# Fused attention and expert layer: the experts' products in a fixed order, the last batch's end and the first expert's entry in smaller pieces

## The chip, the core and the metric

The kernel runs on one core of one Trainium2 chip. Times are device microseconds of one execution; the metric is the median over several executions. The core's engines run side by side and wait for each other through semaphores: PE (TensorE, the matrix products; its weight loads are shown apart as PEld), DVE (VectorE), ACT (ScalarE), POOL (GpSimd) and SP (SyncE, which here only issues transfers). Transfers run on 16 DMA engines.

## What is computed

Attention over 8 batches with 8 heads, 576 positions and 64 numbers per head, masked by blocks of 64, and behind it a layer of 8 experts. Each of the 4608 tokens goes to the expert with the largest logit; of an expert's tokens only the 80 with the largest gate are kept, and all other output rows are zero.

```python
scores = 1.0 / np.sqrt(D) * np.matmul(q, k.transpose(0, 1, 3, 2))
scores = np.where(block_i >= block_j, scores, -1e9)
attn = np.exp(scores - scores.max(-1, keepdims=True))
attn = attn / (attn.sum(-1, keepdims=True) + 1e-09)
x = np.matmul(attn, v).transpose(0, 2, 1, 3).reshape(B * S, H * D)
...
logits = x @ w_gate
expert_idx = np.argmax(logits, axis=1)
gate_w = softmax(logits)[np.arange(N), expert_idx]
for e in range(E):
    tok_idx = np.where(expert_idx == e)[0]
    if len(tok_idx) > capacity:
        keep = np.argpartition(-gate_w[tok_idx], capacity)[:capacity]
        tok_idx = tok_idx[keep]
    h = np.maximum(x[tok_idx] @ w1[e], 0.0)
    out[tok_idx] = gate_w[tok_idx, None] * (h @ w2[e])
```

## The kernel before

The attention takes two heads (a pair) at a time, 32 turns in all. Four pairs make a batch. What each turn issues on each engine is written out by hand in the lists `TURN`, and for the last turn `LAST` (lines 40 and 139): scores on PE, row maxima on DVE, exponentials on ACT, transposes of the probabilities on PE (`back`, in the groups A, B and C), copies out of the PSUM banks (`take`), and the products with v (`values`, lines 683 to 707), which go to the tiles `V0` (eight of nine blocks) and `V1`. The results of four pairs lie transposed in `xT`. `flip` turns them into `Y`, which SP stores to DRAM, and `logits_of` (line 399) multiplies them with the gate's weights, on four column groups of PE at once. `logits_out` copies the logits with ACT, `logits2` transposes them, `products` multiplies them with the reciprocal softmax sums and adds over the heads, `shift`, `expo`, `first_of` and `weight` find each token's expert and gate, and `turn`, `turn2` and `placed` write the gates by expert into `Wt`. For earlier batches this runs beside the next turns. For the last one it stands by itself (lines 829 to 863).

Then DVE takes the largest gates of each partition and half (`MAX8`, line 889). PE spreads them within an expert (line 913), DVE counts for one half how many are larger (line 958), ACT for the other (line 961), which gives each candidate its slot. One-hot tiles `OH` (line 966) and products with the row numbers (line 979) give a table `gi`, by which POOL gathers the rows of each expert (`xg`, line 993).

Per expert, `prepare` divides the rows by their sums (line 1091, four pieces on DVE), transposes them on PE (line 1111) and copies them with ACT (line 1112). `first` makes the first layer (line 1102, two halves of 32 products, two records each), `second` the second (line 1155), and POOL scatters the rows to the output (line 1164). The order in which PE gets this part is not written out: the program's scheduler sets it, apart from a chain within each `second`. `finish` computes the gates' table and a check sum that must hold before the first scatter.

`warm` (line 724) issues products that nothing reads, so that PE is not idle: the numbers in `WARM`, 12, 6, 9 and 24 of them, stand behind `turn2` of batches 6 and 7, behind the ranking, and behind the products with the row numbers. SP clears the output with 18 transfers of 512 KB (`clear`): four in each of the last turns, 16 in all, and two more among the weights. Weights come as 16 transfers of 2 MB into nine buffers; three are loaded during the attention, the fourth when the last batch is stored, the fifth to ninth behind the second gather (`fetches[HOLD]`), the rest as buffers come free.

Of the kernel before, what the change touches and what calls it, by code (L numbers as in the profile page):

```python
# [18 lines left out]
P = 128  # L19
BLK = 64  # L20
NT = 5
FW0, FWA, FWC, FWB = 3, 3, 1, 2
WARM = [8, 12, 6, 9, 24]
# [114 lines left out]
LAST_BANKS = {"B": (4, 5), "A": (0, 1), "C": (6, 7), "L": (2,), "av": (3,)}  # L138
# [17 lines left out]
    (0, "take", "C1", "v"),  # L156
    (0, "values"),
# [12 lines left out]
def tile_attn_moe(ctx, tc, q, k, v, w_gate, w1, w2, capacity, out, xs=None, dbg=None):  # L170
# [77 lines left out]
    prod = sm1.tile([P, NT, H, E], F32, name="prod")  # L248
    lgT = sm1.tile([P, NT * P], F32, name="lgT")
# [108 lines left out]
    class Batch:  # L358
# [18 lines left out]
        def flip(self, pr):  # L377

            nc.vector.transpose(self.Y[:, :, pr], self.xT[:, pr])
# [16 lines left out]
        def logits(self):  # L396
            self.logits_out(self.logits_of())

        def logits_of(self):
            lt = banks("g")  # L400
# [7 lines left out]
        def logits_out(self, lt):  # L408
            for c in range(2):
                nc.scalar.copy(lgT[:, BLK + 288 * c:BLK + 288 * (c + 1)], lt[c][:, 0:288])  # L410
# [9 lines left out]
        def products(self):  # L420
            for pr in range(NP):
                iv = self.la[pr // 2][:, 0:BLK * NT].rearrange("p (t r c) -> p t r c", t=NT, r=2)[:, :, pr % 2, 0:2 * E]
                yield nc.vector.tensor_tensor(
                    prod[:, :, 2 * pr:2 * pr + 2], iv.rearrange("p t (s e) -> p t s e", s=2),
# [4 lines left out]
            yield nc.vector.tensor_reduce(self.lg, prod.rearrange("p t h e -> p t e h"), axis=AX.X, op=ALU.add)  # L429
# [21 lines left out]
        def weight(self):  # L451
            vec = nc.vector
            N = NT
            g = sm.tile([P, N], F32, name="g", bufs=2)
# [54 lines left out]

        def turn2(self, tp):  # L510
# [24 lines left out]
    class Pair:  # L535
# [147 lines left out]
        def values(self):  # L683

            (av,), (self.last,) = banks("av", self.where), banks("L", self.where)
            a4 = self.last[:, 4 * BLK:5 * BLK]
            if turns:
# [4 lines left out]
                     (1, 1, 0, 1, None), (1, 2, 1, 2, 2), (2, 2, 2, 6, 4), (3, 3, 3, 6, 5)]  # L692
            for n_, (j, row, b0, b1, c0) in enumerate(steps):
                for h in range(2):
                    r = slice(h * D, (h + 1) * D)
                    nc.tensor.matmul(a4[r] if c0 is None else av[r, BLK * c0:BLK * (c0 + b1 - b0)], lhsT=self.vn[:, h, j, :],  # L696
                                     rhs=self.PT[:, h, row, b0:b1].rearrange("p b r -> p (b r)"),
                                     start=(n_ < 2), stop=False)
            for h in range(2):
                r = slice(h * D, (h + 1) * D)  # L700
                nc.tensor.matmul(a4[r], lhsT=self.vn[0:BLK, h, 2, :], rhs=self.PT[0:BLK, h, 2, 0], start=False, stop=True)  # L701
                nc.tensor.matmul(av[r, 7 * BLK:8 * BLK], lhsT=self.vt[BLK:P, h, :], rhs=self.PT[BLK:P, h, 2, 0],
                                 start=False, stop=True)
            xT = self.bt.xT[:, self.pr].rearrange("p (b r) -> p b r", r=BLK)
            self.out["V0"] = (bass.AP(xT.tensor, xT.offset, [xT.ap[0], [5 * BLK, 2], [1, 4 * BLK]]),
                              av.rearrange("p (i c) -> p i c", i=2))
# [29 lines left out]
    cleared, kept = 0, 2  # L736
# [55 lines left out]
    slots_ = dict(pe=pe, t=t, ta=ta, warm=lambda: warm(START_WARM, banks("L")[0]))  # L792
# [3 lines left out]
    with tc.manual_schedule():  # L796
        warm(WARM[0], banks("g")[0])
        early = loads(FW0)
        for i in range(-LEAD, n):
# [6 lines left out]
            for _ in range(min(4, nz - kept - cleared) if i >= n - 5 else 0):  # L806
# [51 lines left out]
        for g_ in (found, found, found, weighed, found, weighed, weighed):  # L858
            next(g_)
        bt.turn(nc.vector, 2)  # L860
# [45 lines left out]
    for h in (1, 0):  # L906
# [478 lines left out]
```

## Time and profile before

| | before |
|---|---|
| median of 3 runs | 395.24 us (393.61 to 395.93) |
| the profiled execution | 398.6 us |
| span of the profiled execution | 396.9 us |
| PE busy | 374.6 us (94%) |
| DVE, ACT, POOL busy | 279.5, 289.9, 185.0 us |
| moved by DMA | 84.42 MB |

The span runs from the first to the last instruction of the program; the execution's own time is 1.7 us longer. Times within the profile count from the span's start. [...]

### The profile page before, as it was taken

What the parts mean: (1) busy time and instruction counts of PE and PEld (TensorE: products, weight loads), DVE (VectorE), ACT (ScalarE), POOL (GpSimd) and SP (SyncE); (2) the same over time, 40 slices, a digit from 0 to 9 for tenths busy, and PEclk for the clock granted to TensorE, in tenths of its full rate; (3) what the DMA queues carried; (4) which work ended last, traced back from release to release, by engine and by line L of the source; (5) the groups of instructions that cost most, each with busy time, mean ns of one, the idle gap of its engine ahead of it and who ended that gap; (6) DMA issues with size and microseconds to landing.
All of it is one profiled execution on the core that took longest, in us unless ns stands there. A gap on an engine that the chain in (4) does not pass through costs nothing.

```text
span 396.9 us, 15142 instructions
## 1 busy us (share of the span) xinstructions
PE 374.6 (94%) x5963; PEld 254.3 (64%) x5963; DVE 279.5 (70%) x787; ACT 289.9 (73%) x886; POOL 185.0 (47%) x383
## 2 busy tenths in 40 slices
PE   5899999998999999999999999998996999999991
PEld 3666666665766766766676667666675955655541
DVE  5879899997999999999999999999743230100010
ACT  1799999998999999999999999996121223333231
POOL 6246665674965877667695556301146001000010
PEclk9999999999999999999999999999997899999997
DMA  9969999898999999999999998997669999999401
GB/s 124 153 120 191 145 182 176 160 216 106 190 244 174 155 179 195 161 172 197 128 166 220 154 144 192 385 405 223 144 224 274 391 400 397 393 397 390 182 18 40
DMA packets 169919, 84.42 MB, mean 213 GB/s; under 512 B 132573, under 2 KB 151869, under 8 KB 169840
## 3 DMA queue, kind: packets, MB, share of 16 engines
q1 hardware_dynamic: 158352, 61.80, 71.8%
q0 software_dynamic: 9120, 21.27, 23.2%
q8 instruction: 49, 0.80, 1.0%
q10 hardware_dynamic: 2368, 0.30, 0.6%
q14 instruction: 30, 0.25, 0.3%
HBM read 63.21 MB, written 20.33 MB: 211 GB/s over the span
## 4 chain that ended last, share of the span: by engine, by line
PE 81%; DVE 7%; DMA 4%; issue 3%; SPq 1%; ACT 1%; ACTq 0%; POOL 0%; POOLq 0%; DVEq 0%
PE bank L597 20%; PE bank L696 18%; PE bank L678 13%; PE ps L1102 10%; PE av L1155 9%; DMA ld<-in_q_dram 2%; PE bank L403 2%; PE bank L701 2%; SPq L558 1%; PE bank L614 1%; DMA ld<-in_k_dram 1%; DVE raw L633 1%; DVE negm L633 1%; PE bank L417 1%; PE pm L1155 1%
## 5 line engine op out<-in xcount | busy, mean ns | idle before, releaser
L644 ACT ACTIVATE P<-bank,negm 128x512 f32<-128x512 f32 (+3 forms) x320 | 158.4, 584 | 10.4 <-DVE negm L633 8.0
L597 PE MATMUL bank<-T,qt 64*128 64x320 f32 (+3 forms) x512 | 99.4, 496 | 0.6 <-DVE PT L714 0.6
L633 DVE TENSOR_REDUCE negm<-bank 128x1 f32<-128x320 f32 (+2 forms) x192 | 83.5, 473 | 11.1 <-PE bank L623 11.1
L696 PE MATMUL bank<-PT,vn 128*64 128x64 f32 (+3 forms) x1280 | 88.1, 293 | 0.6 <-ACT PT L714 0.6
L714 ACT COPY PT<-bank 128x512 f32<-128x512 f32 x158 | 81.9, 652 | 3.1 <-PE bank L678 2.6
L696 PEld LDWEIGHTS bank<-PT,vn 128*64 128x64 f32 x1280 | 56.3, 137 | 27.1 <-ACT PT L714 5.2
L580 POOL TENSOR_SCALAR qt<-T 128x128 f32<-128x128 f32 (+2 forms) x96 | 31.1, 342 | 88.5 <-DVE T L573 88.5
L644 ACT ACTIVATION_READ_ACCUMULATOR P<-bank,negm 128x1 f32 x256 | 70.6, 277 | 0.0
L678 PEld LDWEIGHTS bank<-ident,P 64*128 64x128 f32 (+1 forms) x1600 | 58.5, 137 | 11.7 <-issue 6.4
L678 PE MATMUL bank<-ident,P 64*128 64x64 f32 (+1 forms) x1600 | 64.1, 225 | 1.1 <-ACT P L644 0.6
L597 PEld LDWEIGHTS bank<-T,qt 64*128 64x128 f32 x512 | 47.9, 187 | 26.5 <-ACT PT L714 15.6
L633 DVE TENSOR_REDUCE raw<-bank 128x1 f32<-128x64 f32 (+1 forms) x128 | 51.6, 441 | 2.5 <-PE bank L597 1.6
L573 DVE STREAM_TRANSPOSE T<-ld 128x576 f32<-128x576 f32 x64 | 49.3, 770 | 5.0 <-DMA ld<-in_q_dram 3.7
L566 POOL DMA_DIRECT2D vn<-in_v_dram x58 | 46.0, 796 | 1.2 <-issue 1.1
L1102 PE MATMUL ps<-xsT,w 128*64 128x80 f32 x1024 | 41.7, 241 | 3.7 <-issue 3.1
L1102 PEld LDWEIGHTS ps<-xsT,w 128*64 128x64 f32 x1024 | 39.2, 143 | 7.7 <-issue 6.3
L1164 POOL DMA_INDIRECT out_dram<-y,si x8 | 7.4, 924 | 77.9 <-DVE y L1159 77.9
L1159 DVE SCALAR_TENSOR_TENSOR y<-av,comb,yt 80x512 f32<-80x512 f32 (+1 forms) x8 | 5.6, 696 | 50.5 <-ACT yt L1158 50.5
L558 POOL DMA_DIRECT2D ld<-in_k_dram x54 | 37.4, 702 | 4.5 <-DMA ld<-in_q_dram 3.1
L1155 PE MATMUL av<-w,hT 128*32 128x512 f32 (+2 forms) x320 | 39.0, 553 | 0.0
L1125 ACT ACTIVATE hT<-ps 128x320 f32<-128x320 f32 x16 | 7.0, 438 | 35.4 <-PE ps L1102 35.4
L1158 ACT ACTIVATE yt<-ps,gfar 32x512 f32<-32x512 f32 (+2 forms) x18 | 11.4, 636 | 24.5 <-PE ps L1155 24.3
(190 smaller groups left out, 437.7 us busy)
## 6 DMA issues: line engine op xcount, KB each, us to landing
w<-in_moe_w_dram SPq DMA_DIRECT2D x13, 2048.0 KB, 20.6
xs<-Y SPq DMA_DIRECT2D x32, 288.0 KB, 6.4
out_dram<-zero SPq DMA_DIRECT2D x18, 512.0 KB, 7.3
ld<-in_q_dram SPq DMA_DIRECT2D x126, 72.0 KB, 5.3
vn<-in_v_dram POOLq DMA_DIRECT2D x58, 128.0 KB, 5.5
ld<-in_k_dram SPq DMA_DIRECT2D x72, 72.0 KB, 5.4
w<-in_moe_w_dram POOLq DMA_DIRECT2D x8, 512.0 KB, 7.4
ld<-in_k_dram POOLq DMA_DIRECT2D x54, 72.0 KB, 6.4
```

The source lines that it names most:

```text
L558: eng.dma_start(self.nat[x][r], (q, k)[x][b, h0 + h, :, 32 * i:32 * i + 32] .rearrange("(g r) d -> r g d", r=32))
L566: eng.dma_start(self.vn[:, h], v[b, h0 + h, 0:512].rearrange("(j p) d -> p j d", p=P))
L573: nc.vector.transpose(t, self.nat[x].rearrange("p g d -> p (g d)"))
L580: nc.gpsimd.tensor_scalar(qb[:, to], tb[:, of], scalar1=SCALE, scalar2=1.0, op0=ALU.mult, op1=ALU.mult)
L597: nc.tensor.matmul(s[h][:, c:c + n], lhsT=q_[:, P * t - BLK:P * t + BLK], rhs=k_[:, 0:n], start=(c == 0 and g != "2"), stop=(g == "1"))
L633: nc.vector.tensor_reduce(to[:, b, h:h + 1], self.s[g][h][:, c:c + n], axis=AX.X, op=ALU.max, negate=True)
L644: nc.scalar.activation(Pt[self.i % 2][u][:, h, c1:c1 + n], self.s[g][h][:, c:c + n], AF.Exp, bias=self.negm[:, t, h:h + 1], scale=1.0, acc ...
L678: nc.tensor.transpose(pt[c][0:cols.stop - cols.start, n_ * BLK:(n_ + 1) * BLK], row[u][r, h, cols], ident[r, r])
L696: nc.tensor.matmul(a4[r] if c0 is None else av[r, BLK * c0:BLK * (c0 + b1 - b0)], lhsT=self.vn[:, h, j, :], rhs=self.PT[:, h, row, b0:b1]. ...
L714: (nc.scalar.copy if (eng or TAKE[x]) == "a" else nc.vector.tensor_copy)(*self.out.pop(x))
L1102: yield nc.tensor.matmul(dst(b)[64 * c:64 * (c + 1)], lhsT=w_[:, a, col:col + 64], rhs=x_[:, a], start=(a == 0), stop=(a == n - 1))
L1155: last = nc.tensor.matmul(to[col:col + s1 - s0, c0:c1], lhsT=hT[:, a, s0:s1], rhs=w_[:, a, c0:c1], start=(a == ends[0]), stop=(a == ends[1 ...
```

## The change

It does these things:

- PE's order in the expert part is fixed: each `first` follows the `second` of two experts before, each `second` follows the `first` of the next expert. The check sum's second product stands behind the first `second`.
- The first expert enters in four pieces: each is divided, transposed and copied into a tile of its own, and the first half of its products goes piece by piece.
- In the last batch the logits of three of four pairs are made before the values; `V0` lies in two banks, copied by ACT and DVE at once; the logits' second half is copied by DVE; `flip` is cut in two. The products are written with the head innermost (`prod_`). Batch 6's `placed` goes to ACT. `turn_gated` multiplies gate and one-hot in another order, and the tile `Gm` of the last batch is written by POOL.
- The ranking begins with the half that DVE counts.
- All 18 clears go into the last turns, up to five each. Of the five weight loads behind the second gather, the third to fifth each wait for the load two before.
- `WARM` is 9, 6, 9 and 21 in place of 12, 6, 9 and 24. A loop that only runs when the check sum fails gets 30 passes in place of 28.

PE at the first expert's entry; `xn` are the divided rows, `xsT` and `x_0` to `x_3` the transposed ones, `ident` marks a transpose. Before:

```order
L724 MATMUL ps_6160<-identr 128x512 x24
L1111 MATMUL pm<-ident,xn 128x80 x4
L1102 MATMUL ps<-xsT,w 64x80 x32
L1111 MATMUL pm<-ident,xn 128x80 x4
L1102 MATMUL ps<-xsT,w 64x80 x32
```

With the change:

```order
L753 MATMUL ps_6171<-identr 128x512 x21
L1181 MATMUL pm<-ident,xn_0_6241 128x80
L1181 MATMUL pm<-ident,xn_1_6242 128x80
L1181 MATMUL pm<-ident,xn_2_6243 128x80
L1144 MATMUL ps<-x_0_6237,w 64x80 x8
L1181 MATMUL pm<-ident,xn_3_6244 128x80
L1157 MATMUL ps<-x_0_6237,w 64x80 x2
L1144 MATMUL ps<-x_1_6238,w 64x80 x8
L1144 MATMUL ps<-x_2_6239,w 64x80 x8
L1144 MATMUL ps<-x_3_6240,w 64x80 x8
L1167 MATMUL pm<-ident,xn 128x80 x4
```

The first eight products need only the first piece, and two products of the second half have moved between them.

PE at the last batch's values (`PT` and `vn`), logits (`wgd`) and their transposes (`lgT`). Before:

```order
L696 MATMUL bank_5875<-PT,vn 64x256 x2
L696 MATMUL bank_5875<-PT,vn 64x192 x2
L701 MATMUL bank_5876<-PT,vn 64x64
L702 MATMUL bank_5875<-PT,vt_147 64x64
L701 MATMUL bank_5876<-PT,vn 64x64
L702 MATMUL bank_5875<-PT,vt_147 64x64
L403 MATMUL bank_5927<-xT,wgd 32x288 x4
L403 MATMUL bank_5928<-xT,wgd 32x288 x4
L417 MATMUL bank_5946<-ident,lgT 128x64
```

With the change:

```order
L404 MATMUL bank_5878<-xT,wgd 32x288 x3
L404 MATMUL bank_5879<-xT,wgd 32x288 x3
L721 MATMUL bank_5886<-PT,vn 64x64 x2
L721 MATMUL bank_5887<-PT,vn 64x256 x2
...
L726 MATMUL bank_5888<-PT,vn 64x64
L727 MATMUL bank_5887<-PT,vt_148 64x64
L404 MATMUL bank_5878<-xT,wgd 32x288
L404 MATMUL bank_5879<-xT,wgd 32x288
L418 MATMUL bank_5955<-ident,lgT 128x64
```

Six of the eight logits products stand ahead of the values now, and two behind.

The diff, cut to its core:

```diff
-WARM = [8, 12, 6, 9, 24]
+WARM = [8, 9, 6, 9, 21]
...
-LAST_BANKS = {"B": (4, 5), "A": (0, 1), "C": (6, 7), "L": (2,), "av": (3,)}
+LAST_BANKS = {"B": (4, 5), "A": (0, 1), "C": (6, 7), "L": (2,), "av": (3, 4), "g": (5, 0)}
...
+    (0, "logits"),
     (0, "values"),
...
-        def flip(self, pr):
-
+        def flip(self, pr, g0=0, g1=S // 32):
+            nc.vector.transpose(self.Y[:, g0:g1, pr], self.xT[:, pr, 32 * g0:32 * g1])
...
+        def logits_of(self, lt, prs=range(NP)):
             for c in range(2):
-                for pr in range(NP):
+                for pr in prs:
...
+        def logits_out(self, lt, cs=range(2), copy=None):
+            for c in cs:
+                (copy or nc.scalar.copy)(lgT[:, BLK + 288 * c:BLK + 288 * (c + 1)], lt[c][:, 0:288])
...
+            by_head = prod if self.b < B - 1 else prod_.rearrange("p t e h -> p t h e")
...
-                    prod[:, :, 2 * pr:2 * pr + 2], iv.rearrange("p t (s e) -> p t s e", s=2),
+                    by_head[:, :, 2 * pr:2 * pr + 2], iv.rearrange("p t (s e) -> p t s e", s=2),
...
-            yield nc.vector.tensor_reduce(self.lg, prod.rearrange("p t h e -> p t e h"), axis=AX.X, op=ALU.add)
+            yield nc.vector.tensor_reduce(self.lg, by_head.rearrange("p t h e -> p t e h"), axis=AX.X, op=ALU.add)
...
+        def turn_gated(self):
+            self.sp = sp = sm.tile([P, E, NT, 8], F32, name="sp", bufs=1)
+            gs = sm.tile([P, NT, 8], F32, name="gs", bufs=1)
+            nc.vector.tensor_tensor(gs, self.g.unsqueeze(2).broadcast_to([P, NT, 8]),
+                                    sameE.unsqueeze(1).broadcast_to([P, NT, 8]), op=ALU.mult)
+            eq = self.eq.rearrange("p t e -> p e t")
+            for s_ in range(2):
+                nc.vector.tensor_tensor(
+                    sp[:, s_:E:2], eq[:, s_:E:2].unsqueeze(3).broadcast_to([P, E // 2, NT, 8]),
+                    gs.unsqueeze(1).broadcast_to([P, E // 2, NT, 8]), op=ALU.mult)
+            nc.gpsimd.tensor_tensor(Gm[:, NT * self.b:NT * (self.b + 1)], self.eq,
+                                    self.g.unsqueeze(2).broadcast_to([P, NT, E]), op=ALU.mult)
...
-            yield nc.vector.tensor_copy(Wt[:, :, :, self.b, :].rearrange("p h t a -> p t a h"),
-                                        self.tp[:, 0:8 * NT].rearrange("p (t a h) -> p t a h", t=NT, h=2))
+            yield (nc.scalar.copy if self.b == B - 2 else nc.vector.tensor_copy)(
+                Wt[:, :, :, self.b, :].rearrange("p h t a -> p t a h"),
+                self.tp[:, 0:8 * NT].rearrange("p (t a h) -> p t a h", t=NT, h=2))
...
+            two = len(avs) > 1
...
+            if two:
+                steps = [y for j, row, b0, b1, c0 in steps for y in (
+                    [(j, row, b0, b0 + 4 - c0, c0), (j, row, b0 + 4 - c0, b1, 4)]
+                    if c0 is not None and c0 < 4 < c0 + b1 - b0 else [(j, row, b0, b1, c0)])]
...
+            if two:
+                self.out.update((f"V0{i}", (self.bt.xT[:, self.pr, 5 * BLK * i:5 * BLK * i + 4 * BLK],
+                                            avs[i][:, 4 * BLK * i:4 * BLK * (i + 1)])) for i in range(2))
...
-    cleared, kept = 0, 2
+    cleared, kept = 0, 0
...
+    def logits():
+        early_logits.extend(banks("g", LAST_BANKS))
+        batches[B - 1].logits_of(early_logits, range(NP - 1))
...
-            for _ in range(min(4, nz - kept - cleared) if i >= n - 5 else 0):
+            for _ in range(min(5, nz - kept - cleared) if i >= n - 5 else 0):
...
-        to, from_ = pairs[n - 1].out.pop("V0")
         pairs[n - 1].take("V1", "v")
-        nc.scalar.copy(to[:, 0], from_[:, 0])
-        nc.vector.tensor_copy(to[:, 1], from_[:, 1])
+        pairs[n - 1].take("V00", "a")
+        pairs[n - 1].take("V01", "v")
...
-        lt = bt.logits_of()
-        pairs[n - 1].flip()
+        bt.logits_of(early_logits, (NP - 1,))
+        bt.flip(NP - 1, 0, S // 64)
+        bt.logits_out(early_logits, (0,))
+        bt.logits_out(early_logits, (1,), nc.vector.tensor_copy)
+        bt.flip(NP - 1, S // 64, S // 32)
-        bt.logits_out(lt)
...
-        bt.turn(nc.vector, 2)
+        bt.turn_gated()
...
-    for h in (1, 0):
+    for h in range(2):
...
+    hot = vec.tensor_tensor(slot[:, 0:NH], cnt_v, pen[:, 0], op=ALU.add)
+    for c0 in range(0, NCAND, 3):
+        if c0 == NH:
+            with tc.issue_after(hot.ins):
+                hot = vec.scalar_tensor_tensor(slot[:, NH:], cnt_a, 0.5, pen[:, 1], op0=ALU.mult, op1=ALU.add)
+        with tc.issue_after(hot.ins):
...
+        parts = finish_()
...
+        yield
+        pc2 = ps_m.tile([P, 512], F32, name="pm")
+        with tc.issue_after(added_[0].ins):
+            nc.tensor.matmul(pc2[:, 0:1], lhsT=ones, rhs=dsb, start=True, stop=True)
         vec.tensor_tensor(nb, nb, pc2[:, 0:1], op=ALU.add)
...
-    weights(1, fetches[HOLD])
-    with tc.issue_after(loaded.ins):
-        while cleared < nz:
-            loaded = clear(cleared, nc.sync)
-            cleared += 1
-    weights(FWA - 2 + FWC + FWB, fetches[HOLD])
+    assert cleared == nz or ov is None
+    behind = [fetches[HOLD], fetches[HOLD]]
+    for _ in range(FWA - 1 + FWC + FWB):
+        weights(1, behind.pop(0))
+        behind.append(loaded.ins)
...
+        if pieces is not None:
+            for a in range(n):
+                pieces(a, after)
+                for b in range(nb):
+                    for c in range(2):
+                        col = (2 * b + c) * 64
+                        with ExitStack() as order:
+                            if after is not None:
+                                order.enter_context(tc.issue_after(after.ins))
+                            after = nc.tensor.matmul(dst(b)[64 * c:64 * (c + 1)], lhsT=w_[:, a, col:col + 64],
+                                                     rhs=x_[a], start=(a == 0 and b == 0),
+                                                     stop=(a == n - 1 and b == nb - 1))
+                yield after
+            return
...
+    def prepare_pieces():
+        x_ = [fx.tile([P, CHUNK], F32, name=f"x0_{a}") for a in range(KP)]
+        xn = [fx.tile([CHUNK, P], F32, name=f"xn0_{a}") for a in range(KP)]
+        divide(xn, xg[0])
+        def turn_(a, after):
+            tp = ps_m.tile([P, 512], F32, name="pm")
+            with ExitStack() as order:
+                if after is not None:
+                    order.enter_context(tc.issue_after(after.ins))
+                nc.tensor.transpose(tp[:, 0:CHUNK], xn[a], ident[0:CHUNK, 0:CHUNK])
+            nc.scalar.copy(x_[a], tp[:, 0:CHUNK])
+        def pieces(a, after):
+            for a_ in range(3) if a == 0 else range(a + 2, min(a + 3, KP)):
+                turn_(a_, after)
...
+        turned_[e] = last
...
-        last = None
+        last = turned_[min(e + 1, E - 1)]
...
+        added_[e] = last
...
+        pieces = None
+        if e == 0:
+            xs_[0], pieces = prepare_pieces()
+        elif e + 1 < E:
+            ready(e + 1)
...
-            hT_[e] = first(e, xs_[e], (lambda: ready(1)) if e == 0 else None)
+            hT_[e] = first(e, xs_[e], (lambda: ready(1)) if e == 0 else None, added_.get(e - 2), pieces)
...
-            finish(divided_[2])
+            rest = finish(divided_[2])
...
-            scatter(e - 1, second(e - 1, hT_[e - 1]))
+            y = second(e - 1, hT_[e - 1])
+            for _ in rest if e == 1 else ():
+                pass
+            scatter(e - 1, y)
```

## Rows read from the trace of the kernel before

**Rows 1.** The page, busy time of each engine

```profile
PE 374.6 (94%) x5963; PEld 254.3 (64%) x5963; DVE 279.5 (70%) x787; ACT 289.9 (73%) x886; POOL 185.0 (47%) x383
```

**Rows 2.** Timeline of PE, last batch: start us, us, engine, line, op, out<-in, xcount [idle before]

```profile
274.59 2.75 PE L696 MATMUL bank<-PT,vn 128*64 128x320 f32 x40 [0.63 <-ACT PT L714]
...
277.95 1.34 PE L403 MATMUL bank<-xT,wgd 128*32 128x288 f32 x16 [0.33 <-DVE xT L714]
```

**Rows 3.** Timeline of PE, first experts

```profile
292.03 5.73 PE L724 MATMUL ps<-identr 128*128 128x512 f32 x24
...
298.56 2.06 PE L1102 MATMUL ps<-xsT,w 128*64 128x80 f32 x43 [0.52 <-ACT xsT L1112]
301.77 0.29 PE L1102 MATMUL ps<-xsT,w 128*64 128x80 f32 x2 [1.16 <-issue]
...
304.63 1.35 PE L1102 MATMUL ps<-xsT,w 128*64 128x80 f32 x16 [0.41 <-issue]
...
306.63 4.09 PE L1102 MATMUL ps<-xsT,w 128*64 128x80 f32 x64
...
311.08 4.65 PE L1102 MATMUL ps<-xsT,w 128*64 128x80 f32 x128
```

**Rows 4.** Waits of PE, 296 to 320: line, releaser, us in total, times, longest

```profile
PE ps L1102 <- issue: 3.1, 4, 1.2
```

**Rows 5.** Stretches: us, busy PE, PEld, DVE, ACT, POOL (records), granted clock, DMA share, GB/s

```profile
302.00:304.00 2.00, 0.49 (x4) 0.38 (x3) 0.00 (x0) 0.00 (x0) 1.60 (x5) 0.82 1.05 408
...
306.00:310.00 4.00, 4.00 (x54) 3.83 (x56) 0.89 (x4) 0.86 (x2) 0.00 (x0) 0.50 1.04 334
...
360.00:370.00 10.00, 10.00 (x223) 7.53 (x217) 0.74 (x1) 3.35 (x6) 0.91 (x1) 1.00 1.04 388
370.00:380.00 10.00, 10.00 (x145) 4.88 (x143) 0.75 (x1) 2.92 (x5) 0.91 (x1) 1.00 0.22 76
```

**Rows 6.** DMA queues (transfers, MB, share): the page, then 303 to 305

```profile
q8 instruction: 49, 0.80, 1.0%
...
q8 instruction: 1, 0.02, 3.0%
```

**Rows 7.** Timeline of DVE, last batch to first expert

```profile
269.23 1.40 DVE L633 TENSOR_REDUCE negm<-bank 128x1 f32<-128x320 f32 x4
...
280.31 0.68 DVE L423 TENSOR_TENSOR prod<-bank,rs 128x80 f32<-128x80 f32 x4 [0.96 <-PE bank L417]
281.03 0.82 DVE L429 TENSOR_REDUCE lg<-prod 128x40 f32<-128x320 f32 x1
...
282.24 0.22 DVE L521 COPY Wt<-bank 128x40 f32<-128x40 f32 x1
...
288.25 0.42 DVE L958 TENSOR_SCALAR_CACHE_REDUCE junk<-av,key 128x192 bf16<-128x192 f32 x1 [0.95 <-PE av L913]
...
290.48 1.36 DVE L966 TENSOR_TENSOR OH<-slot,iota_s 128x240 bf16<-128x240 f32 x4
...
296.52 0.89 DVE L1091 TENSOR_TENSOR xn<-xg 80x128 f32<-80x128 f32 x4 [4.13 <-DMA xg<-xs,gi]
```

**Rows 8.** Timeline of ACT, ranking and first expert

```profile
287.41 0.42 ACT L961 ACTIVATE junk<-ps,keyn 128x192 bf16<-128x192 f32 x1 [4.82 <-DMA xs<-Y]
...
289.71 0.23 ACT L961 ACTIVATION_READ_ACCUMULATOR junk<-ps,keyn 128x1 f32 x1
...
298.08 0.43 ACT L1112 COPY xsT<-pm 128x320 f32<-128x320 f32 x1 [5.50 <-issue]
```

**Rows 9.** Timeline of SP's transfers

```profile
246.53 20.11 SPq L239 DMA_DIRECT2D out_dram<-zero  x16
...
277.72 0.38 SPq L387 DMA_DIRECT2D xs<-rs  x1
...
283.56 15.19 SPq L337 DMA_DIRECT2D w<-in_moe_w_dram  x2
```

**Rows 10.** Chain that ended last: start us, us, what

```profile
378.15 0.44 PE pm L1155 x2
```

More of the change, by code (lines that the diff above doesn't have):

```diff
@@ L683, in values @@
         def values(self):
-            (av,), (self.last,) = banks("av", self.where), banks("L", self.where)
+            avs, (self.last,) = banks("av", self.where), banks("L", self.where)
+            two = len(avs) > 1
             a4 = self.last[:, 4 * BLK:5 * BLK]
@@ L692, in values @@
                      (1, 1, 0, 1, None), (1, 2, 1, 2, 2), (2, 2, 2, 6, 4), (3, 3, 3, 6, 5)]
+            first = {2: two}
+            if two:
+                steps = [y for j, row, b0, b1, c0 in steps for y in (
+                    [(j, row, b0, b0 + 4 - c0, c0), (j, row, b0 + 4 - c0, b1, 4)]
+                    if c0 is not None and c0 < 4 < c0 + b1 - b0 else [(j, row, b0, b1, c0)])]
+            low = [n_ for n_, x in enumerate(steps) if x[4] is not None and x[4] < 4][-1] if two else None
             for n_, (j, row, b0, b1, c0) in enumerate(steps):
@@ L1060, in finish_ @@
         vec.tensor_reduce(nb, pc[:, E:E + 2], axis=AX.X, op=ALU.add)
-        pc2 = ps_a.tile([P, 512], F32, name="av")
-        nc.tensor.matmul(pc2[:, 0:1], lhsT=ones, rhs=dsb, start=True, stop=True)
+        yield
+        pc2 = ps_m.tile([P, 512], F32, name="pm")
+        with tc.issue_after(added_[0].ins):
+            nc.tensor.matmul(pc2[:, 0:1], lhsT=ones, rhs=dsb, start=True, stop=True)
         vec.tensor_tensor(nb, nb, pc2[:, 0:1], op=ALU.add)
@@ L1112, in prepare, with first @@
         nc.scalar.copy(x_.rearrange("p a s -> p (a s)"), tp[:, 0:KP * CHUNK])
-        return x_, last
-    def first(e, x_, then=None):
+        return [x_[:, a] for a in range(KP)], last
+    def prepare_pieces():
[4 more added lines that the diff above has]
+            tp = ps_m.tile([P, 512], F32, name="pm")
+            with ExitStack() as order:
+                if after is not None:
+                    order.enter_context(tc.issue_after(after.ins))
+                nc.tensor.transpose(tp[:, 0:CHUNK], xn[a], ident[0:CHUNK, 0:CHUNK])
[3 more added lines that the diff above has]
+                turn_(a_, after)
+        return x_, pieces
+    def first(e, x_, then=None, after=None, pieces=None):
         hT = fx.tile([P, FP, CHUNK], F32, name="hT", bufs=3)
@@ L1119, in first @@
             ph = ps_s.tile([P, 512], F32, name="ps")
-            for last in blocks(lambda b: ph[:, b * CHUNK:(b + 1) * CHUNK], w_[:, :, 512 * f:512 * (f + 1)], x_, KP, 4):
+            for last in blocks(lambda b: ph[:, b * CHUNK:(b + 1) * CHUNK], w_[:, :, 512 * f:512 * (f + 1)], x_, KP, 4,
+                               None if f else after, None if f else pieces):
                 pass
@@ L1151, in second @@
                                         (far[i][1], rest[far[i][0]], FAR, (NEAR, FP - 1)))
-                    with ExitStack() as order:
-                        if last is not None:
-                            order.enter_context(tc.issue_after(last.ins))
+                    with tc.issue_after(last.ins):
                         last = nc.tensor.matmul(to[col:col + s1 - s0, c0:c1], lhsT=hT[:, a, s0:s1], rhs=w_[:, a, c0:c1],
@@ L1210, in tile_attn_moe @@
         step = 1.0
-        for it in range(28):
+        for it in range(30):
             vec.tensor_scalar(mid, lo, scalar1=step, scalar2=None, op0=ALU.add)
```

59 lines of the change are left out of this document (25 added, 34 removed).

## The prediction

> **What bounds the kernel now.** I read the page first: PE is busy for 374.6 of 396.9 us [rows 1], so only time in which PE does nothing useful, or works slowly, can be won. Up to 274 us the change leaves PE's order alone, so I went on to the timeline of PE from the last batch to the first experts. There the reader should see two things. First, a chain without overlap: the last values products (from 274.59), the logits (277.95), their transposes, DVE's choice of an expert, the ranking, the gather, and the 24 filling products that only keep PE working (292.03 to 297.76) [rows 2, 3]. The first product of an expert starts at 298.56. Second, that this expert runs badly. Its 128 matmul records should take what the next expert's 128 take, 4.65 us. They take 7.42 (298.56 to 305.98) and 4.09 for the two halves of 64 [rows 3]. Against 2.32 for each half that is 5.10 + 1.77 = 6.9 us lost.
>
> The waits of PE say that 3.1 us of it are four gaps with no releaser that the profile shows ("issue") [rows 4]. [...] The DMA engines, meanwhile, are full (share 1.05) from 302. The queue view offers a suspect: the queue of kind "instruction" moved 49 transfers, 0.80 MB, so 16 KB each, and one of them falls into 303 to 305, where the gaps end; the same view of 283 to 303 lists none [rows 6]. From 311 PE is dense to the end (10.00 of 10 us at 360 to 370). The weights are not what it waits for: the DMA share falls to 0.22 at 370 to 380 [rows 5], so the last weights land near 372, and the last expert's products on them begin at 378.15 [rows 10], some 6 us later.
>
> **The change part by part.** Shifts are us earlier (+) or later (-) for the first expert.
>
> Early logits. Three of four head pairs' logits, 12 of 16 records, move ahead of the values. The 16 took 1.34 us, so 12 cost about 1.0. PE stands idle 0.63 us there, waiting for ACT's copy of PT; about 0.4 sticks out and moves the values [rows 2]. Behind the values only two logits products remain, but both write the same 32 rows of their banks, and I count them one after the other, so the second half is no earlier relative to the values. The transposes go into banks of their own now: four of ten no longer wait for the second copy, 0.15 to 0.2 gained. DVE's copy of the second half stands between two halves of the flip, and the second flip ends before the transposes do. Net -0.2 (bounds -0.5 and +0.2).
>
> The products of the last batch are written with the head innermost. The sum over heads read every eighth number and took 0.82 us for 320 numbers; a reduction of 320 neighbours took 0.35 (1.40 for four) [rows 7]. That is +0.45 if writing costs nothing, and 0 if the four products (0.68 together) pay what the sum saves; I take +0.25. [...]
>
> The copy of batch 6's places goes from DVE to ACT: its row has 0.22 us there, half of it beside the next one [rows 7], +0.1. ACT is idle there. The product with the gate is not removed from DVE: gs takes the place of Gm, so 0; Gm itself goes to POOL, where nothing waits for it.
>
> Ranking: the half that DVE counts goes first. ACT's six counts run from 287.41 to 289.92, 2.5 us [rows 8]; they now start where DVE's started, at 288.25 [rows 7], 0.84 later, and end near 290.8. Then one short add and two of the four one-hot steps (1.36 for four [rows 7]) remain, to 291.65 in place of 291.84: +0.2. Three fewer filling products before it lie in idle time: 0.
>
> First expert's entry. Before: DVE divides four pieces 296.52 to 297.41, four transposes, one ACT copy of 320 columns 298.08 to 298.51, first product 298.56 [rows 3, 7, 8]. Now 21 filling products end 0.7 earlier, near 297.05; the first transpose follows, its copy of 80 columns takes about 0.2 (between the 0.43 for 320 columns and nothing), and the first product starts near 297.55. The other pieces are divided and copied beside the eight products of the piece before. +1.0 (bounds 0.6 and 1.1).
>
> Order of the experts. Products and transposes stay the same in number; the pc2 product and the transposes only change place. PE is dense there before, and in the new order each product's operands come at least one block of 4.65 us ahead: 0. The one block that comes late enough to matter is the check sum behind the first second-layer block; only POOL's scatter waits for it: 0.
>
> Clears and weights. The two clears leave their place behind the second load and join the sixteen, which took 20.11 us from 246.53; two more cost SP 2.5 us, ahead of batch 6's stores. The last batch's stores began at 277.72, released by DVE, and nothing before them is waited for: 0 [rows 9]. Among the weights stands 1 MB less. The last three of the five loads now each wait for the load two before, so at most two are in flight; one always is, so the DMA engines stay fed: 0 on PE, with 6 us of slack.
>
> Sum without the stall: 0.2 lost, 0.25 + 0.1 + 0.2 + 1.0 won, 1.35 us (bounds 0.3 and 2.2). The profiled execution took 398.6, so 397.3 if the stall stays as it is.
>
> The stall. It is 6.9 us as it stands. If the gaps come because that 16 KB transfer queues behind what SP issued (a load issued by 298.75 [rows 9], then 1 MB of clears, then four more loads), the change takes away the clears and holds three of the loads back. It goes, or shrinks below half; gone, 398.6 - 1.35 - 6.9 = 390.4.
>
> How this stands to the median: the profiled execution is 3.4 us above it. If profiling costs that everywhere, the two results become 387.0 and 393.9. If ordinary runs simply have a shorter stall, the first stays 390.4. The three runs lie 2.3 apart, which fits a stall of changing length. I take the middle for a stall that is gone, 388.7, and with some of it left 389.5.
>
> **The rivals.** *The stall stays (393.9).* For it: the first product and the place of the gaps, some 43 records into the block [rows 3], move together with the load that waits for the second gather, and two loads, 4 MB, still stand in the queue. Against it: the bulk issued next to it is gone. [...]
>
> *The transfers come too late twice (400.8, slower).* PE has 5963 loads and 5963 matmuls [rows 1] for 49 transfers, about 243 instructions each. At full pace 128 instructions pass in 2.32 us [rows 3], a transfer's worth in 4.4. The first expert and the next now run 256 matmul records without the pause. If the transfer after the late one needs more than 4.4 us in full DMA, PE stops a second time and the clock falls longer: another 6.9 on 393.9. Against it: in before the block from 311.08 ran at full pace in full DMA traffic.
>
> *The change does only its small steps and PE waits for weights.* That would need the hold to lose over 6 us of DMA time; I give it no share of its own.
>
> **How the numbers follow.** Stall gone or under half: 0.48, 389.5 (its own range 386.5 to 392). Stall stays: 0.37, 393.9 (392.5 to 396). Two stops or another new wait: 0.15, about 400. A measurement can tell about 0.5%, 2 us: below 393.3 is faster, above 397.2 slower. Faster: 0.48 and a third of the second case, 0.61; same 0.24; slower 0.15. The range takes the first two cases, 386.5 to 396.0.
>
> **What would show it.** Right: the first half of the first expert's products takes under 4.5 us, the second 2.3; no wait "issue" over 0.6 us; the granted clock stays at 1.00 from 298 to 312; the first product starts 1.0 to 1.7 us earlier; the last one 8 us earlier. Wrong: the same gaps at the same count of records, the clock at 0.50 after them, or PE waiting for "w". The early logits are mis-sized if the values move by more than 0.6, the layout if sum and products together save under 0.1.

## The result and the profile after

| | before | after |
|---|---|---|
| median of 4 runs each, side by side | 394.43 us (392.31 to 395.93) | 390.61 us (388.82 to 391.97) |
| ratio after / before | | 0.9894, 95% interval 0.9848 to 0.9941 |
| the profiled execution | 398.6 us | 390.77 us |
| its span, mean granted clock (a share of full speed) | 396.9 us, 0.985 | 389.1 us, 0.996 |

Here and below a ratio leaves out the executions that lie over 1.5% above the fastest of their kernel, so it is not quite the quotient of the medians.

The change is faster by 1.1%, and the range of the forecast (389.5, from 386.5 to 396.0) holds the time. The profiled executions differ by 7.8 us, though, and the medians by 3.8, so the two profiles can't be the whole story; the experiments show why.

The last back transposes on PE before the change (columns as in [rows 2]):

```profile
272.36 1.60 PE L678 MATMUL bank<-ident,P 64*128 64x64 f32 x33 [0.32 <-DVE xT L714]
```

The timeline of PE after the change, from there on:

```profile
272.98 1.59 PE L695 MATMUL bank<-ident,P 64*128 64x64 f32 x33 [0.33 <-DVE xT L743]
274.50 1.17 PE L404 MATMUL bank<-xT,wgd 128*32 128x288 f32 x12
275.60 2.77 PE L721 MATMUL bank<-PT,vn 128*64 128x64 f32 x48
...
292.79 5.01 PE L753 MATMUL ps<-identr 128*128 128x512 f32 x21
297.64 0.66 PE L1181 MATMUL pm<-ident,xn 80*128 80x80 f32 x3
298.24 0.78 PE L1144 MATMUL ps<-x,w 128*64 128x80 f32 x16
...
299.35 1.83 PE L1144 MATMUL ps<-x,w 128*64 128x80 f32 x48
...
301.54 2.29 PE L1157 MATMUL ps<-x,w 128*64 128x80 f32 x60
...
304.19 4.65 PE L1157 MATMUL ps<-xsT,w 128*64 128x80 f32 x128
...
311.69 0.61 PE L1230 MATMUL av<-w,hT 128*32 128x512 f32 x2 [0.44 <-issue]
```

Against the row before and [rows 3] the last back transposes begin 0.6 us later here (272.98 for 272.36). PE's order ahead of them is unchanged, and over the profiles of this document they begin anywhere from 269.8 to 275.4, so I measure from them. The first product of an expert comes 25.26 us behind them, and came 26.20 behind: 0.94 gained. Then the gaps are gone: from the first expert's first product to the second expert's block it takes 5.95 us (298.24 to 304.19) in place of 12.52 (298.56 to 311.08).

The stretches (columns as in [rows 5]) show the clock at 1.00 where it had been at 0.82 (302 to 304) and at 0.50 (306 to 310):

```profile
302.00:304.00 2.00, 2.00 (x57) 1.91 (x54) 0.90 (x4) 0.19 (x2) 1.70 (x2) 1.00 0.96 355
304.00:306.00 2.00, 2.00 (x56) 1.91 (x56) 0.00 (x0) 0.72 (x2) 1.67 (x8) 1.00 1.06 330
306.00:308.00 2.00, 2.00 (x65) 2.00 (x62) 0.03 (x1) 0.44 (x1) 0.35 (x1) 1.00 1.06 270
```

And DVE (columns as in [rows 7]) shows the new layout and the new ranking:

```profile
281.19 0.79 DVE L425 TENSOR_TENSOR prod__112<-bank,rs 128x80 f32<-128x80 f32 x4
282.01 0.48 DVE L431 TENSOR_REDUCE lg<-prod__112 128x40 f32<-128x320 f32 x1
...
291.67 0.17 DVE L1009 SCALAR_TENSOR_TENSOR slot<-cnt_a,pen 128x6 f32<-128x6 f32 x1 [0.43 <-ACT junk L997]
291.87 0.73 DVE L1002 TENSOR_TENSOR OH<-slot,iota_s 128x240 bf16<-128x240 f32 x2
```

One difference stood in no term of the sum: the end. Behind the last scatter the program jumps over the fallback code that runs only when the check sum fails. These are the instructions at that jump, before and then after (line, engine's sequencer, operation, count: duration in ns min/median/max, start of the first and the last in us):

```profile
L1197 PEldq EVENT_SEMAPHORE  x2: 51/51/51, 391.9 to 395.6; - x2
...
L1197 PEldq COMPARE_BRANCH  x1: 3498/3498/3498, 388.4 to 388.4; - x1
```

```profile
L1279 PEldq EVENT_SEMAPHORE  x2: 51/51/51, 385.9 to 386.1; - x2
...
L1279 PEldq COMPARE_BRANCH  x1: 3378/3378/3378, 382.5 to 382.5; - x1
```

Before, PE's two semaphore instructions behind the jump stand 3.6 us apart, and SP waits 2.25 us for the second; the trace's transfers show a 16 KB instruction transfer (queue q8) from 392.66 to 394.14, between them. After, they stand 0.15 us apart. These are POOL's last scatters, before and after:

```profile
390.02 0.91 POOL L1164 DMA_INDIRECT out_dram<-y,si  x1 [3.23 <-DVE y L1159]
```

```profile
384.12 0.91 POOL L1240 DMA_INDIRECT out_dram<-y,si  x1 [3.87 <-DVE y L1234]
```

From the end of the last scatter's issue to the end of the span it takes 4.03 us in place of 5.95. After the change the end waits only for POOL, whose DRAIN behind the scatter takes 3.06 us (385.17 to 388.23); before, that one ended at 394.14, and PE's second semaphore came 1.44 us later.

So the 7.82 us between the spans are: 0.61 later at the last back transposes, 0.94 up to the first product, 5.60 in the experts (first product to last product 90.07, now 84.47: 6.57 gained in the first expert, 0.97 lost behind it), and 1.92 at the end, less 0.02 between the last product and the last scatter.

### The profile page after: what moved, and what is told of

It reads as the page before. It is cut to its first block, busy times and chain, and to the rows that moved or that the text cites. A ratio compares the mean times of both kernels' runs of the same rounds, so it can differ in the third digit from the quotient of the medians.

```text
span 389.1 us, 15153 instructions
## 1 busy us (share of the span) xinstructions
PE 370.9 (95%) x5965; PEld 249.8 (64%) x5965; DVE 280.5 (72%) x788; ACT 289.8 (74%) x889; POOL 185.2 (48%) x384
## 4 chain that ended last, share of the span: by engine, by line
PE 85%; DVE 5%; DMA 3%; ACT 3%; issue 1%; SPq 1%; ACTq 0%; POOL 0%; POOLq 0%; DVEq 0%
PE bank L614 21%; PE bank L721 20%; PE bank L695 13%; PE av L1230 10%; PE ps L1157 9%; PE bank L404 2%; PE bank L726 2%; ACT P L661 2%; DMA ld<-in_q_dram 2%; PE bank L631 1%; PE ps L753 1%; DMA ld<-in_k_dram 1%; DVE raw L650 1%; PE pm L1230 1%; PE bank L418 1%
## 5 line engine op out<-in xcount | busy, mean ns | idle before, releaser
L661 ACT ACTIVATION_READ_ACCUMULATOR P<-bank,negm 128x1 f32 x256 | 68.8, 269 | 0.0
L1230 PE MATMUL av<-w,hT 128*32 128x512 f32 (+2 forms) x320 | 40.0, 554 | 0.4 <-issue 0.4
L1157 PE MATMUL ps<-xsT,w 128*64 128x80 f32 x896 | 32.5, 233 | 0.0
L1157 PEld LDWEIGHTS ps<-xsT,w 128*64 128x64 f32 x896 | 31.4, 137 | 1.4 <-ACT yt L1233 0.9
L1230 PE MATMUL ps<-w,hT 128*32 128x512 f32 (+2 forms) x72 | 29.3, 548 | 0.0
```

What stands on the lines that cost most here:

```text
L661: nc.scalar.activation(Pt[self.i % 2][u][:, h, c1:c1 + n], self.s[g][h][:, c:c + n], AF.Exp, bias=self.negm[:, t, h:h + 1], scale=1.0, acc ...
L1157: last = nc.tensor.matmul(dst(b)[64 * c:64 * (c + 1)], lhsT=w_[:, a, col:col + 64], rhs=x_[a], start=(a == 0), stop=(a == n - 1))
L1230: last = nc.tensor.matmul(to[col:col + s1 - s0, c0:c1], lhsT=hT[:, a, s0:s1], rhs=w_[:, a, c0:c1], start=(a == ends[0]), stop=(a == ends[1 ...
```

## The experiments

Three comparisons of four kernels (experiments 1 to 4, 5 to 8, 9 to 12), each on a chip of its own, with the kernel before in it. Two theories for the gaps: the transfers that SP issues delay PE's instructions (the prediction's), or the gaps belong to something else, the entry's order or the chip, and the change's profile lacks them for that reason.

**1. The change with the old clears and loads.**

```diff
-cleared, kept = 0, 0
+cleared, kept = 0, 2
...
-    behind = [fetches[HOLD], fetches[HOLD]]
-    for _ in range(FWA - 1 + FWC + FWB):
-        weights(1, behind.pop(0))
-        behind.append(loaded.ins)
+    weights(1, fetches[HOLD])
+    with tc.issue_after(loaded.ins):
+        while cleared < nz:
+            loaded = clear(cleared, nc.sync)
+            cleared += 1
+    weights(FWA - 2 + FWC + FWB, fetches[HOLD])
```

> The change, but with the clears and the weight loads of the kernel before: two clears behind the second load, and the last four loads waiting for the second gather alone. If the DMA traffic delays the 16 KB instruction transfer, the gaps come back: first half of the first expert's products over 5 us, issue waits of PE over 2 us, the granted clock 0.5 after them, a profiled time near 396 and a median 3 to 5 us above the change's 390.6. If the gaps went because the entry and the products' order changed, the first half stays near 2.9 us and the median within 1 us of 390.6.

Measured: 395.24 us beside 397.08 for the kernel before, ratio 0.9939 (0.9907 to 0.9971). The gaps are back: six waits "issue", 3.6 us in all, the first product at 298.36, the second expert's block at 311.89. Taken alone this speaks for the prediction.

**2. The kernel before with the new clears and loads** (the same edit the other way round).

> The kernel before with only the clears (all eighteen early) and the weight loads (at most two in flight) of the change. If DMA traffic makes the gaps, they go: first half of the first expert near 2.4 us, clock 1.00 at 304 to 310, profiled time 391 to 393, median 2 to 4 us under the kernel before. If the entry and the order did it, the gaps stay as in [rows 3] and the median is that of the kernel before within 1 us.

Measured: 398.37 us, ratio 1.0007 (0.9963 to 1.005). The gaps stay (six, 3.1 us). Holding the transfers does not remove them.

**3. The kernel before, again.**

> The kernel before, unchanged. If the stall belongs to the program, its profile shows again four gaps of about 0.9 us near record 43 of the first expert and the clock at 0.5 for 306 to 310, and again a time near 398. If it varies by execution, the first half of the first expert takes under 4 us in this profile, and the time is nearer to 394.

Measured: 400.85 us, with six gaps of 3.3 us in all. In the first comparison all 29 executions of the kernel before have a mean granted clock of 0.990 or less, as profiles with gaps have (0.983 to 0.988), where the change's profile has 0.996.

**4. The change with the old entry** (`ready(0)` in place of `prepare_pieces()`).

> The change with the first expert's entry in one piece again (one tile, four transposes, one copy of 320 columns, the 64 products by output block). By the sum of the prediction the first product starts 0.8 to 1.0 us later than in the change and the median rises by 1.0 (bounds 0.6 and 1.1), to 391.6. If the entry's order is what removed the gaps, they come back and the median rises by 3 to 5.

Measured: 396.0 us, ratio 0.9957 (0.9917 to 0.9996). The first product comes 26.00 us behind the start of the last back transposes, against 25.26: the entry is worth 0.74. The gaps are here too (four, 4.0 us; a fifth wait "issue", 0.51 us ahead of the first product, is the one for the copy of 320 columns, 0.52 in [rows 3]), so neither the entry nor the loads is told apart by the first comparison; a chip on which the kernel before always has them may give them to every version.

**5. The kernel before with gathers 2 to 7 held** behind the last product of the first half.

```diff
+    gather(range(2))
...
+    def midway(last):
+        gather(range(2, E), last)
+        ready(1)
```

> The kernel before, but POOL issues the gathers of experts 2 to 7 only once the last product of the first expert's first half is done. In the four profiles with gaps PE runs again 1.3 to 1.5 us after POOL's last gather ends. If the gathers make the gaps, the first half now takes 2.4 us and the gaps come later (256 instructions on) or not at all, clock 1.00 at 304 to 308. If they don't, the gaps stand at the same place, some 40 records into the first half, for 3 to 5 us.

Measured: 396.88 us, ratio 1.0066 (1.0031 to 1.0101). The first half runs through in 2.43 us; one gap comes in the second half, 1.16 us long, while the held gathers are issued:

```profile
296.68 2.43 PE L1109 MATMUL ps<-xsT,w 128*64 128x80 f32 x64 [0.52 <-ACT xsT L1119]
299.04 0.50 PE L1118 MATMUL pm<-ident,xn 80*128 80x80 f32 x4
299.47 3.53 PE L1109 MATMUL ps<-xsT,w 128*64 128x80 f32 x94
304.16 3.67 PE L1109 MATMUL ps<-xsT,w 128*64 128x80 f32 x98 [1.16 <-issue]
309.29 0.59 PE L1032 MATMUL ps<-RG,OH 128*80 128x24 bf16 x12 [1.46 <-POOL RG L947]
```

The last row is the price: POOL is late with what `finish` needs, and PE waits for it. The second comparison ran on another chip, though, and there the kernel before has a clock of 0.993 or more in 10 of 25 executions, so one profile without the gaps in their old place proves little.

**6. The kernel before with loads and clears held** behind the first half.

> The kernel before, but SP issues the five weight loads and the two clears behind the first expert's first half, so that nothing of SP is in the queue while that half runs. If bulk transfers delay PE's instructions, the gaps go (first half 2.4 us, clock 1.00) and may come again behind the loads; the median falls by up to 2 us or more. If the gaps stay at the same count of records for 3 us or more, bulk transfers are not what makes them.

Measured: 406.3 us, ratio 1.0303 (1.0243 to 1.0362). The first expert runs without a gap, and one of 0.9 us comes near 312; but now PE waits 6.4 and 1.9 us for weights. Taken alone, the missing gap would speak for the prediction, but by the clock four in ten executions of the kernel before lack it on this chip. The loads go out only 2.75 us later against the last back transposes (28.74 us behind their start, before 25.99), and PE, without gaps, reaches the second expert's block 7.0 us earlier (31.74 for 38.72). So the 6 us of slack that the prediction saw in the loads are not there: in the kernel before SP's wait for the last load ends at 374.5, and the first product on it begins at 378.08, 3.6 us later.

**7. The change, again.**

> The change, unchanged, beside the same runs of the kernel before. If its missing stall belongs to the program, its profile shows again a first half of 2.9 us, clock 1.00 from 298 to 312, and its median lies 5 us or more under that of the kernel before where that one stalls (395 to 398). If it varies by execution, the mean clock of its runs scatters down to 0.985 to 0.988, as in the runs with gaps.

Measured: 390.05 us beside 394.08, ratio 0.9888 (0.985 to 0.9926). The profiled execution took 1994 us, with every matmul several times as long as elsewhere; nothing is read from it. Eight of the other ten have a clock of 0.995 or more and a median of 389.54; the ten of the kernel before with 0.993 or more have 393.08. Where by that clock neither has the gaps, 3.5 us are left.

**8. The change with unheld loads, clears early.**

```diff
-        weights(1, behind.pop(0))
-        behind.append(loaded.ins)
+    weights(FWA - 1 + FWC + FWB, fetches[HOLD])
```

> The change with the five loads not held (all wait for the second gather alone), the clears early as in the change. If holding the loads is what keeps the gaps away, they are back: first half over 5 us, mean clock near 0.988, median 3 to 5 us above the change. If the two clears were what brought them back in the first experiment, the first half takes 2.9 us and the median is the change's within 1 us.

Measured: 390.25 us, ratio 0.9905 (0.9865 to 0.9945), the change's time. Seven of nine executions have a clock of 0.995 or more, and the profile has no gap in the first expert. Without the hold the loads cost nothing here. What it does have is one wait "issue" of 1.1 us, at the product where the change has its 0.44:

```profile
310.23 0.61 PE L1227 MATMUL av<-w,hT 128*32 128x512 f32 x2 [1.09 <-issue]
```

**9. The change with all logits behind the values.**

```diff
-    (0, "logits"),
...
-        bt.logits_of(early_logits, (NP - 1,))
+        early_logits = banks("g", LAST_BANKS)
+        bt.logits_of(early_logits)
```

> The change with all sixteen logits products of the last batch behind the values again (same banks, same copies and flips). From the end of the last back transposes to the first expert's product the change takes 23.66 us, the kernel before 24.60. If the early logits cost 0.2 to 0.4 here, as the profile after the change suggests, this stretch falls to 23.3 to 23.5; if they gain, it grows to 23.9 or more. The median stays within 1 us of the change's.

Measured: from the end of the last back transposes to the first product it takes 23.27 us, in the change 23.67, so the early logits cost 0.40. The median is 394.83, ratio 0.9941 (0.9904 to 0.9978); it is the lowest of its comparison, though the intervals overlap.

**10. The change with the old layout.**

> The change with the last batch's products in the old layout (number of the expert innermost, the sum reads every eighth number). By the term of the prediction the stretch from the last back transposes to the first expert's product grows by 0.25, to 23.9 us, with the four products back at 0.68 and the sum at 0.82. If the layout is worth nothing, it stays at 23.66.

Measured: the same stretch takes 23.88 us, so the layout is worth 0.21. DVE's rows return to those of [rows 7]:

```profile
278.02 0.69 DVE L425 TENSOR_TENSOR prod<-bank,rs 128x80 f32<-128x80 f32 x4
278.74 0.80 DVE L431 TENSOR_REDUCE lg<-prod 128x40 f32<-128x320 f32 x1
```

The median is 397.64, ratio 0.9993 (0.9946 to 1.0041).

**11. The change with 28 rounds in the fallback.**

> The change with 28 rounds again in the skipped fallback loop. It also stands for the change in this comparison, since nothing ahead of the end differs. From the end of the last scatter's issue to the end of the span the kernel before takes 5.95 us, the change 4.03; in the kernel before PE's two semaphore instructions behind the skipped code stand 3.6 us apart, in the change 0.15. If the two added rounds moved that place off a block's edge, the tail is 5.5 to 6.2 us here and the median 1.9 above the change's; if the instructions added elsewhere did it, the tail stays at 4.0 to 4.2. If the change removes the stall also where the kernel before has it in all runs, the mean clocks here are over 0.992 while those of the kernel before are 0.985 to 0.99.

Measured: 397.9 us beside 398.11, ratio 0.9995 (0.9953 to 1.0036). The tail is 4.12 us and the two semaphores stand 0.15 us apart (396.1 to 396.2), so the two added rounds are not what shortened it. And the gaps are all there, in a program that is the change itself up to the last scatter:

```profile
301.78 0.86 PE L1144 MATMUL ps<-x,w 128*64 128x80 f32 x19
303.67 0.31 PE L1144 MATMUL ps<-x,w 128*64 128x80 f32 x2 [1.03 <-issue]
305.12 0.30 PE L1144 MATMUL ps<-x,w 128*64 128x80 f32 x2 [1.14 <-issue]
306.54 0.36 PE L1144 MATMUL ps<-x,w 128*64 128x80 f32 x4 [1.12 <-issue]
307.97 1.66 PE L1144 MATMUL ps<-x,w 128*64 128x80 f32 x21 [1.07 <-issue]
```

```profile
306.00:308.00 2.00, 0.39 (x5) 0.37 (x5) 0.00 (x0) 0.23 (x1) 1.76 (x6) 0.81 1.07 377
308.00:310.00 2.00, 2.00 (x24) 1.83 (x24) 0.00 (x0) 0.33 (x1) 0.79 (x4) 0.50 1.05 283
```

SP issues nothing between 302.2 and 314.0 here: two loads are in flight, the other three are held. All 12 executions have a clock of 0.988 or less. The change does not remove the gaps; whether a run has them depended on the comparison it belongs to, and so perhaps on the chip. The version may count as well: in the second comparison the change and experiment 8 have a clock of 0.995 or more in 15 of 19 executions, the kernel before 0.993 or more in 10 of 25. No run tells which part of the change would do that.

**12. The change with held loads, clears late.**

> The change with its held loads, but with the two clears behind the first of them, as before. If the two clears are what brings the gaps back, the first half of the first expert takes over 5 us here and the mean clock is 0.985 to 0.99 in most runs, against over 0.992 in the run with 28 rounds beside it. If the clears don't matter, clocks and median (but for the tail) are those of that run within 1 us.

Measured: 396.4 us, ratio 0.997 (0.9925 to 1.0015), gaps of 3.9 us. Beside experiment 11, which has them without the late clears, it tells nothing of the clears.

## Where the gaps start and end

Nine profiles have the gaps (before, and experiments 1 to 4 and 9 to 12). In all nine the first gap comes 258 to 266 PE instructions (products, weight loads and waits) after the start of the 16 KB instruction transfer that falls between 278 and 285 us. Counted from the start of the program, 9166 to 9172 PE instructions stand ahead of it, in either version. PE runs again, behind the last gap, 1.28 to 1.49 us after POOL's last gather has been issued. In experiment 11 this is POOL's row:

```profile
305.63 0.96 POOL L1027 DMA_INDIRECT xg<-xs,gi  x1 [0.30 <-issue]
306.59 0.21 POOL L1055 CAST gp<-cand 128x12 bf16<-128x12 f32 x1
```

The gather ends at 306.59, and PE's 21 products begin at 307.97. The trace has 12,102 PE instructions before and 12,107 after, and 49 transfers of 16 KB, so 247 for each. From the start of the first of them to that of the 35th, the last ahead of the gaps (18.51 to 282.52 us before the change), 8677 PE instructions start, and 8679 after the change: 255 for each. So the gaps, 258 to 266 instructions behind the 35th, fit the edge of such a block of instructions; that a transfer brings PE's next block is an inference from these counts alone. The waits at this edge are 3.1 to 4.4 us in the nine profiles. The transfer alone doesn't explain them: in experiment 1 it lands at 300.75 and the gaps go on to 305.66.

The other four profiles have one wait "issue" further on: experiment 5 behind 9410 instructions, the change and experiments 6 and 8 behind 9665, one and two blocks after the place of the gaps. These waits are of another kind. Each ends 1.38 to 1.54 us after a 16 KB transfer has landed (in the change it lands at 310.31 and PE runs at 311.69), much as the first instruction behind the jump at the end does (1.37 to 1.54 us in all thirteen profiles). That fits a block that came late itself, at a price of 0.44 to 1.16 us.

That the gathers make the gaps is argued, not shown. For it: the end, nine times; experiment 5, where the first crossing, near 298.1, has no gather beside it and no gap. The gap at its next crossing is no evidence, since it ends as the late blocks do (transfer landed at 302.76, PE at 304.16), with two gathers still to be issued. Against it: after the change, and in experiments 6 and 8, PE crosses while POOL gathers (in the change at about 300.0, with gathers from 294.04 to 304.05) without a gap. What makes one chip have the gaps in nearly every execution and another in some stays open.

## Why the prediction was right, and where not

The time was right by a sum of errors on both sides, and so in part by luck. In the profiles the small steps gave 0.94 us up to the first product, where 1.35 were predicted; the experts gave 5.60, where the stall stood for 6.9; and 1.92 came from the end, for which there was no term. The prediction's signs of a stall that is gone nearly all appear after the change (first half 2.94 us, second 2.29, longest wait "issue" 0.44, clock 1.00 from 298 to 312). They show that this execution had no gaps, and not why.

- **The stall.** The step that failed: "If the gaps come because that 16 KB transfer queues behind what SP issued [...] the change takes away the clears and holds three of the loads back. It goes, or shrinks below half". Experiments 2 and 11 have the held transfers and the full gaps (3.1 and 4.4 us), and experiment 8 has neither the hold nor a gap in the first expert. The rival by which the stall stays was right for experiments 2 and 11; that the stall stays in every execution of the change was not so. That its time (393.9) is not the measured one goes with the next two points.
- **The size of the stall in the median.** 6.9 us was read from one execution with gaps. Experiment 7's comparison has executions of the kernel before without them. If the 0.94 up to the first product and the 1.92 at the end hold in the other executions too, about 1 of the 3.8 us between the medians is left, which these rows don't assign; a profile of the kernel before without gaps was not taken.
- **The end.** No term stood for it, and the prediction says nothing of the jump. In the profiles it is the largest gain outside the experts, 1.92. All five profiles of the kernel before and its variants have the two semaphores 3.25 to 3.72 us apart and a tail of 4.9 to 6.2 behind the scatter; all eight of the change have 0.15 to 0.22 and 3.9 to 4.2, with 28 rounds too. That the instructions added ahead move the pair off a block's edge fits this; no run moved them alone.
- **Early logits.** Predicted -0.2, measured -0.40 (experiment 9), inside the bounds. The values begin 2.62 us behind the last back transposes, before 2.23; the second half of `flip` ends with the transposes, so nothing returns.
- **Layout.** Predicted +0.25, measured +0.21. The four products rose from 0.68 to 0.79, the sum fell from 0.82 to 0.48. The reading by which the strided writes would pay all of it back (0) is ruled out.
- **Ranking and places.** Predicted +0.3, measured about -0.1: from DVE's maximum (281.89 before, 282.53 after) to the gather's indices (292.22 and 292.98) it takes 10.33 and 10.45. ACT's counts were put second and now end last: DVE waits 0.43 for them.
- **Entry.** Predicted +1.0, measured +0.74 by experiment 4; from the start of the division to the first product it is 2.04 before and 0.97 after, 1.07 gained. Experiment 4 keeps the 21 filling products, so 0.74 of this belong to the four pieces.
- **Order of the experts.** Predicted 0. From the second expert's block to the last product it takes 77.4 to 78.3 us in the change's six versions with gaps (experiments 1, 4 and 9 to 12) and 77.55 to 77.7 before and in experiments 2 and 3: 0 within 0.7. In the change's own profile it is 78.52, and 79.17 in experiment 8: without gaps in the first expert, a later wait appears (0.44 and 1.09), which ends as those at the late blocks do. That is the rival of a second stop, at 1.0 and 1.6 us in place of 6.9; the clock stays at 1.00.
- **Weights.** The 6 us of slack were read from the fall of the DMA share at 370 to 380; by SP's wait for the last load they were 3.6 us (see experiment 6). The term itself, 0, holds: PE has no wait for a load after the change.
- **With the gaps in both**, the entry's gain is lost: the gaps end behind the gathers, which come no earlier, so the earlier start only lengthens them (first product to second expert's block 14.07 in experiment 11, 12.52 and 12.96 in the two profiles of the kernel before). From the start of the last back transposes to the second expert's block it takes 38.7 to 39.6 us in the change's versions with gaps, and 38.7 to 39.2 before. In that comparison the change's program (experiment 11) has a ratio of 0.9995, with an interval that reaches from 0.5% faster to 0.4% slower, against 0.9888 in the comparison of experiment 7. Its profile has the short end (4.12 us), but a gain of 1.9 us would lie at the edge of that interval; the medians there differ by 0.2 us.

## What to carry to other kernels

Look at a stall in more than one execution before its whole length goes into a sum: here the change had it in the profile from one chip (experiment 11, the same program up to the last scatter) and not in its own, and two profiles differed by twice what the medians did. Read the end of the program as well, down to the semaphores behind the last jump; two us were there that no view of the busy engines shows. And give a step its gain only if what it feeds comes earlier too: an earlier first product was worth nothing where the gaps behind it ended no earlier.

## What the runs showed of the hardware

- In the gaps PE starts its products in steps of about 0.715 us or twice that (in experiment 1 at 301.35, 302.78, 303.50, 304.22, 304.95, 305.66), a few products a step. The pause costs a second time: in experiment 1 PE is busy 0.62 and 0.53 us of the two stretches from 300 to 304, and from 304 to 310 the granted clock is 0.50; the 60 products of the second half that follow take 3.52 us (from 308.02), in the change 2.29 at 1.00.
- The jump over the fallback code takes PE 3.3 to 3.9 us in thirteen profiles, with a 16 KB transfer within it; ACT, DVE, POOL and SP jump there in 50 to 76 ns. In the kernel before the first semaphore instruction runs 1.43 us after that transfer has ended (390.52 to 391.95). The second runs 1.44 us after the next has (394.14 to 395.58), 3.64 us behind the first; in the change, with no transfer between them, it is 0.15.
- Writing the products with the head innermost cost 0.11 us over four products (0.79 for 0.68); reading them with a stride of eight had cost 0.34 in one sum of 320 numbers (0.82 for 0.48).
